# An attention and mixture-of-experts kernel: attention's instruction order written out as a list, and some of its steps moved between engines

## The chip, the cores and the metric

One Trainium2 chip, one of its cores. The metric is device time in microseconds from start to end of one execution, in the median of several runs. The engines named below are PE (TensorE, matrix products and transposes), DVE (VectorE), ACT (ScalarE), POOL (GpSimd) and SP (which here issues most DMAs). Each engine runs its own instructions in program order, and engines wait for one another by semaphores.

## The reference

Two stages. Attention with a memory term, for 8 batches of 8 heads, 576 positions and 64 columns; then a mixture of experts whose tokens are assigned by one global sort.

```python
scores = scale * np.matmul(q, k.transpose(0, 1, 3, 2))
scores = np.where(causal, -1000000000.0, scores)
scores = scores - scores.max(-1, keepdims=True)
a = np.exp(scores)
a /= a.sum(-1, keepdims=True) + 1e-09
local = np.matmul(a, v)
def phi(x):
    return np.where(x > 0, x, np.exp(x) - 1.0) + 1.0
q_p = phi(q)
mem_ret = np.einsum('bhsd,bhde->bhse', q_p, M_prev)
mem_norm = np.einsum('bhsd,bhd->bhs', q_p, z_prev)[..., None] + 1e-06
mem_out = mem_ret / mem_norm
g = 1.0 / (1.0 + np.exp(-beta))[None, :, None, None]
return (g * mem_out + (1 - g) * local).astype(np.float32)
```

The MoE then takes the 4608 rows of 512 columns, gives each to one of 8 experts (at most 576 rows an expert, in the order of the logits) and computes `np.maximum(x[mask] @ w1[e], 0.0) @ w2[e]`.

## The kernel before

Attention works in 16 units, each half a batch: four heads of 576 positions, held as 18 blocks of 128 rows for k, q and phi(q). Most values are kept as two fp16 halves, a high half (a rounded copy) and a low half (what the copy lost), so that a product of two such values is several fp16 matmuls. For each unit `attention` adds steps to a planner:

- loads of k, q, v and M by SP (`lk`, `lq`, `lv`, `lm`);
- `turned` for k, q and phi(q): the high half (`kh`, `qh`, `ph`; a cast of 1152 columns), the low half (`kl`, `ql`, `pl`; a subtraction), transposes on PE into a PSUM bank, and their evacuation to the tiles kT, qT and pT by DVE or ACT (`te`);
- `kb` and `qmove`: copies of kT and qT to other partitions, by DMA;
- `maxes`: raw scores of each block of rows, and their row maxima under the causal mask. Before, DVE adds a mask and takes the maximum in one instruction (`Q`, line 1067, with an accumulator read) for tiles of 512, 384, 256 and 128 columns, and a plain reduction (`R`, line 1066) where no mask is needed; the maxima of a unit are transposed on PE (`mfin2`), copied (`mfin2r`) and moved into the tile qM by DMA (`mfin3`);
- phi(q) in the tile ef: `phr` (a ReLU of -q), `phe` (the exponential, ACT, in place, line 1138), `phs` (max(q, 0) plus it, DVE, line 1139);
- `mz`: z copied into the last column of the M tile mf (line 1142), then M's high and low halves (`mh`, `mh2`, `ml`);
- `vh`, `vl`: v's halves in the tile V;
- `scores`: scores with the maxima subtracted (`S`, PE), exponentials by ACT (`Eh`, `Ef`, `E`), low halves of the exponentials by DVE or POOL (`P2v`, `P2`), products with v and with M (`AV1` to `AV3`, `AVm`), the division and the sum of both terms (`N0` to `N3`, `nadd`), and the result's high and low halves (`ncast`, `nsub`) in the tile xs, which SP stores to HBM and transposes for the logits (`fin`).

Five PSUM banks (`pb`) are shared by transposes, maxima, scores and logits of all units; a step that takes a bank waits for the one that lets it go. The planner `Sched.run` goes through all steps once while the program is made: each has a duration, a priority (the large table `PR`) and one or more engines that may do it, some pinned by `PR['pin']`; it takes at each point the step that can start first, and the resulting order is the order of instructions on every engine. `LK` names steps that are held not to overlap between DVE and POOL; it is used by the planner alone. The MoE (`moe_all`) has a planner run of its own with the table `PM`.

`cp` copies on a chosen engine, and its lines are those of ACT (933), DVE (934) and POOL (935).

Of the kernel before, what the change touches and what calls it, by code (L numbers as in the profile page):

```python
# [23 lines left out]
 'dl': {'0': {'AV': -2321.92,  # L24
              'MX': 1567.76,
              'N': -24421.58,
              'P2': -4357.96,
              'S': 101.14,
              'fin1': 22868.1,
              'fin2': 10356.86,  # L30
              'kb': 10286.06,
              'kh': -45730.44,
              'kl': 20174.46,
              'kt': -4701.95,
              'lk': -12408.59,
              'lm': -8436.44,
              'lq': -2541.36,
              'lv': -3.36,
              'maxrem': 3733.37,
              'mfin': 29276.67,  # L40
              'mfin2': -10538.29,
              'mfin3': 7506.77,
              'mh': -11209.39,
              'ml': -432.1,
              'mz': 12658.92,
              'nadd': -11907.02,
              'ncast': -7225.71,
              'nsub': -10647.97,
              'ph': -1228.79,
              'phe': -9589.46,  # L50
              'phr': 524.92,
              'phs': 2230.42,
              'pl': 4308.28,
              'proc24': 3267.06,
              'pt': 11255.13,
              'qh': -4155.4,
              'ql': 7002.13,
              'qmove': -223.83,
              'qt': 10808.21,
              'sj4': 22053.16,  # L60
              'vh': -293.15,
              'vl': -4289.79},
        '1': {'AV': -11630.65,
              'MX': 5085.57,
              'N': -6291.91,
              'P2': -3722.96,
              'S': 0.29,
              'fin1': 18360.27,
              'fin2': -6498.84,
              'kb': -13149.86,  # L70
              'kh': -9834.86,
              'kl': -14831.77,
              'kt': 2765.98,
              'lk': -26.17,
              'lm': -31.5,
              'lq': -62.5,
              'lv': 65.33,
              'maxrem': 241.19,
              'mfin': 827.99,
              'mfin2': 5904.98,  # L80
              'mfin3': 8067.82,
              'mh': -6693.41,
              'ml': -3921.85,
              'mz': 12321.27,
              'nadd': 28446.8,
              'ncast': -5424.62,
              'nsub': -11693.87,
              'ph': 492.03,
              'phe': 2716.39,
              'phr': -7873.98,  # L90
              'phs': -15036.85,
              'pl': 8602.27,
              'proc24': -8298.99,
              'pt': 9687.89,
              'qh': 27462.53,
              'ql': -726.83,
              'qmove': -2093.73,
              'qt': -7770.46,
              'sj4': 1.71,
              'vh': -3758.76,  # L100
              'vl': -4489.33},
        '10': {'AV': 2861.92,
               'MX': 0.01,
               'N': -4207.12,
               'P2': -7603.6,
               'S': -0.44,
               'fin1': -11796.22,
               'fin2': 2697.91,
               'kb': -6760.73,
               'kh': -7032.06,  # L110
               'kl': 9191.09,
               'kt': -2885.08,
               'lk': -23037.77,
               'lm': -3438.56,
               'lq': -2491.39,
               'lv': -3392.66,
               'maxrem': 7.99,
               'mfin': -13621.83,
               'mfin2': -3709.75,
               'mfin3': -12679.91,  # L120
               'mh': 4128.87,
               'ml': 4639.23,
               'mz': -8635.19,
               'nadd': 14785.77,
               'ncast': 20932.03,
               'nsub': 12672.19,
               'ph': 3299.99,
               'phe': -9809.36,
               'phr': -20534.33,
               'phs': -933.81,  # L130
               'pl': 8303.64,
               'proc24': 9747.88,
               'pt': -5727.95,
               'qh': 56.16,
               'ql': -21808.29,
               'qmove': -6139.71,
               'qt': 813.03,
               'sj4': -16488.77,
               'vh': 2047.99,
               'vl': -16738.43},  # L140
        '11': {'AV': -11203.75,
               'MX': 0.6,
               'N': 14876.06,
               'P2': -700.32,
               'S': 0.11,
               'fin1': -8124.01,
               'fin2': -3919.93,
               'kb': 9923.63,
               'kh': 12644.97,
               'kl': -13145.41,  # L150
               'kt': -4241.87,
               'lk': -6151.58,
               'lm': -7286.77,
               'lq': 7551.39,
               'lv': 7510.93,
               'maxrem': 2.79,
               'mfin': 22015.1,
               'mfin2': 6463.64,
               'mfin3': -7945.76,
               'mh': -9010.16,  # L160
               'ml': 7934.19,
               'mz': -3520.69,
               'nadd': 2187.16,
               'ncast': 12966.79,
               'nsub': -4987.87,
               'ph': 4067.79,
               'phe': 16439.48,
               'phr': -16517.7,
               'phs': 7862.4,
               'pl': 3996.54,  # L170
               'proc24': 2350.4,
               'pt': -0.15,
               'qh': 1067.34,
               'ql': 512.84,
               'qmove': -18712.55,
               'qt': -9981.91,
               'sj4': -4091.57,
               'vh': -11967.99,
               'vl': -5668.57},
        '12': {'AV': 13431.14,  # L180
               'MX': -0.34,
               'N': 6485.25,
               'P2': -2957.52,
               'S': 0.54,
               'fin1': -4378.18,
               'fin2': 23705.86,
               'kb': -1628.06,
               'kh': -4672.12,
               'kl': 9427.26,
               'kt': -3533.86,  # L190
               'lk': -3255.11,
               'lm': 3597.42,
               'lq': 2527.1,
               'lv': 5090.06,
               'maxrem': 0.14,
               'mfin': -7530.28,
               'mfin2': -24054.29,
               'mfin3': -4992.24,
               'mh': 2100.24,
               'ml': 10776.14,  # L200
               'mz': -6507.17,
               'nadd': 6833.95,
               'ncast': -7937.44,
               'nsub': -4335.52,
               'ph': -18163.77,
               'phe': -21792.72,
               'phr': 5627.57,
               'phs': -4855.84,
               'pl': -1558.07,
               'proc24': -9941.83,  # L210
               'pt': -18765.17,
               'qh': 5798.81,
               'ql': -1106.61,
               'qmove': 10262.54,
               'qt': -7534.44,
               'sj4': -7761.78,
               'vh': -14193.73,
               'vl': -14434.34},
        '13': {'AV': -8356.88,
               'MX': -0.87,  # L220
               'N': -7818.18,
               'P2': 5237.25,
               'S': -1.37,
               'fin1': -6282.38,
               'fin2': -13271.62,
               'kb': -7142.61,
               'kh': 3724.27,
               'kl': 3441.14,
               'kt': 9439.61,
               'lk': 2207.4,  # L230
               'lm': 10938.95,
               'lq': 4829.3,
               'lv': -23324.49,
               'maxrem': 5.14,
               'mfin': 4464.01,
               'mfin2': -357.39,
               'mfin3': 4612.32,
               'mh': -2791.23,
               'ml': -11716.33,
# [636 lines left out]
def attention(ctx,tc,q,k,v,M_prev,z_prev,beta,wg,xd,L1,NB,cst,rcst):  # L876
# [98 lines left out]
    def one(nm,alts,f,p,**kw): return SC.add(nm,alts,f,prio=c0+p,**kw)  # L975
# [799 lines left out]
```

## Time and profile before

| | |
|---|---|
| median of three runs | 911.14 us (910.07 to 912.41) |
| the profiled execution | 910.64 us, its span 908.8 us |
| mean granted TensorE clock | 0.959 |
| busy over the span: PE, DVE, ACT, POOL | 803.3, 670.7, 580.7, 543.7 us |
| attention, search, MoE | 0 to about 437, to about 480, to the end |

Busy times are unions of the drawn intervals. A matmul's end is modelled, and successive matmuls overlap, so PE's busy time is not its work. In the groups, the first number behind the bar is the busy time of a group in us, the second the mean of one instruction in ns, and then comes the idle time of the engine just ahead of these instructions with what ended it.

### The profile page before, as it was taken

The numbers are of one execution on the slowest core, as the hardware profiler recorded it, in microseconds if no ns is written. First come the engines' busy times: TensorE is split into PE (matmuls) and PEld (weight loads), VectorE is DVE, ScalarE is ACT, GpSimd is POOL, SyncE is SP. The second block draws the span as 40 slices with busy tenths as digits, with TensorE's granted clock in tenths as the row PEclk, the third lists the DMA queues.
The fourth block names the chain that finished last, engine by engine and source line by source line (L and its number), as shares of the span: only waits on it lengthen the run. The fifth ranks groups of instructions, "written<-read, shape, count | busy, mean of one in ns | idle before, by whom it ended". The sixth has DMA issues, their size and how long they took to land.

```text
span 908.8 us, 24389 instructions
## 1 busy us (share of the span) xinstructions
PE 803.3 (88%) x9240; PEld 526.2 (58%) x9240; DVE 670.7 (74%) x2507; ACT 580.7 (64%) x1027; POOL 543.7 (60%) x564
## 2 busy tenths in 40 slices
PE   3687998999999899999226999999999999999995
PEld 2475887777787688888115445454444444444442
DVE  8798898999999899997788878787867774111020
ACT  4767787887898888976226674848383846552120
POOL 5776886887898786866104492928174646852101
PEclk9999899999999999999557999999999999999998
DMA  5566777765757566334124455566463828940001
GB/s 127 117 142 132 166 155 156 165 149 127 161 130 168 120 139 136 86 71 92 48 93 146 164 144 195 143 213 148 167 168 124 226 89 208 248 150 18 35 13 41
DMA packets 231755, 120.86 MB, mean 133 GB/s; under 512 B 199509, under 2 KB 208725, under 8 KB 231637
## 3 DMA queue, kind: packets, MB, share of 16 engines
q1 hardware_dynamic: 225749, 100.42, 45.2%
q0 software_dynamic: 5888, 18.88, 6.7%
q8 instruction: 72, 1.18, 0.5%
q14 instruction: 46, 0.38, 0.1%
HBM read 72.40 MB, written 18.87 MB: 100 GB/s over the span
## 4 chain that ended last, share of the span: by engine, by line
PE 49%; DVE 22%; issue 12%; DMA 6%; POOL 5%; ACT 3%; SPq 2%; another core or an unknown queue 0%; POOLq 0%; DVEq 0%; ACTq 0%
PE py L1417 15%; PE ph L1417 15%; PE pb L892 7%; PE avo L892 5%; DVE pb L1067 4%; DVE scr L1658 2%; DVE xt L1264 2%; DMA xT<-xs 2%; PE pb L1052 2%; PE prem L1417 2%; DVE pl L1210 2%; SPq L959 1%; POOL h L1043 1%; PE pr L1417 1%; DMA qM<-qT 1%
## 5 line engine op out<-in xcount | busy, mean ns | idle before, releaser
L1574 POOL TENSOR_TENSOR wl<-wst,wh 128x1024 f16<-128x1024 f32 x62 | 131.3, 2140 | 80.8 <-ACT wh L1573 59.5
L1417 PE MATMUL ph<-xT,wh 128*128 128x512 f16 (+1 forms) x560 | 162.9, 364 | 2.8 <-DVE hl L1617 1.4
L1067 DVE CUSTOM_DVE_ANT_0 pb<-pb,maskF 128x128 f32<-128x128 f32 (+3 forms) x256 | 124.7, 497 | 7.4 <-PE pb L892 3.7
L892 PE MATMUL pb<-qT,kT 128*128 128x64 f16 (+3 forms) x576 | 106.1, 245 | 8.2 <-DVE mx L1067 1.8
L1636 POOL DMA_INDIRECT out_dram<-ys,idx x40 | 38.9, 973 | 119.1 <-ACT ys L1631 99.8
L1205 ACT ACTIVATE ph<-pb 128x512 f16<-128x512 f32 x144 | 86.0, 597 | 29.1 <-PE pb L892 23.0
L1617 DVE SCALAR_TENSOR_TENSOR hl<-ph,hh 128x512 f16<-128x512 f32 x64 | 44.0, 688 | 80.2 <-ACT hh L1616 77.2
L1417 PEld LDWEIGHTS <-wh 128*128 128x128 f16 x1072 | 68.4, 98 | 59.6 <-issue 3.5
L892 PE MATMUL pb<-qM,kB 128*128 128x64 f16 (+3 forms) x576 | 99.2, 244 | 1.7 <-DMA qM<-mr 1.7
L1417 PE MATMUL py<-wh,hh 128*128 128x512 f16 x256 | 97.0, 379 | 1.5 <-ACT hh L1616 1.1
L1417 PE MATMUL ph<-xT,wl 128*128 128x512 f16 (+1 forms) x280 | 97.7, 363 | 0.0
L1417 PE MATMUL py<-wl,hh 128*128 128x512 f16 x256 | 97.0, 379 | 0.0
L1417 PE MATMUL prem<-xT,wh 128*128 128x64 f16 x512 | 96.3, 193 | 0.0
L1658 DVE TENSOR_SCALAR_CACHE_REDUCE scr<-p_LwT,th 128x320 f16<-128x320 f32 x168 | 85.1, 543 | 2.7
L1616 ACT ACTIVATE hh<-ph 128x512 f16<-128x512 f32 x64 | 38.0, 593 | 76.2 <-PE ph L1417 55.5
L892 PE MATMUL pb<-kT,qM 128*128 128x512 f16 (+5 forms) x384 | 77.6, 314 | 8.8 <-DVE mx L1067 3.4
L1417 PEld LDWEIGHTS <-hh 128*128 128x128 f16 x512 | 47.3, 97 | 56.2 <-ACT hh L1616 1.3
L1656 ACT ACTIVATE scs<-p_LwT,th 128x320 f16<-128x320 f32 x84 | 47.0, 560 | 50.7 <-DVE th L1665 40.2
L892 PE MATMUL avo<-V,ph 128*128 128x65 f16 x1344 | 78.7, 194 | 0.0
L892 PE MATMUL avo<-V,pl 128*128 128x65 f16 x672 | 74.9, 196 | 0.0
L892 PEld LDWEIGHTS <-ph 128*128 128x128 f16 x1344 | 70.6, 98 | 5.1 <-issue 0.9
L1496 POOL DMA_INDIRECT xg<-xd,idx x40 | 38.6, 964 | 51.6 <-DVE sa L1517 35.0
(304 smaller groups left out, 2358.3 us busy)
## 6 DMA issues: line engine op xcount, KB each, us to landing
wst<-in_moe_w_dram SPq DMA_DIRECT2D x32, 1024.0 KB, 7.7
kf<-in_k_dram SPq DMA_DIRECT2D x64, 128.0 KB, 2.8
qf<-in_q_dram SPq DMA_DIRECT2D x64, 128.0 KB, 2.8
xd<-xs SPq DMA_DIRECT2D x16, 512.0 KB, 3.5
vf<-in_v_dram SPq DMA_DIRECT2D x48, 128.0 KB, 2.8
kB<-kT SPq DMA_DIRECT2D x15, 288.0 KB, 3.4
qM<-qT SPq DMA_DIRECT2D x15, 288.0 KB, 5.5
vF<-in_v_dram SPq DMA_DIRECT2D x16, 128.0 KB, 3.1
```

The lines of the kernel that those rows point to most:

```text
L892: def MM(*a,**kw): mm(*a,skip_group_check=True,**kw)
L1052: for i in range(a,b_): nc.tensor.transpose(p[:,128*(i-a):128*(i-a)+128],g()[:,i],cst['idh'])
L1067: Q=lambda o,i,n: nc.vector.tensor_tensor_reduce(out=i,in0=i,in1=cst['maskF'][:,512-n:512],scale=1.0,scalar=-3e38,op0=ALU.add,op1=ALU.max, ...
L1205: c=SC.add('Eh',[('A',478)],lambda x,a=a: nc.scalar.activation(phs_[x.buf['ph']][:,0:512],pbb[a.buf['pb']],AF.Exp,scale=0.125),acq=('ph',) ...
L1417: def MM(*a,**kw): mm(*a,skip_group_check=True,**kw)
L1496: SC.add('gather',[('P',1250 if i<4 else 1200,'p',0,(1250,'n'))],lambda x: G_.indirect_dma_start(out=xg[0:r_,i],out_offset=None,in_=xd,in_ ...
L1574: SC.add('sp',[('P',2079)],lambda x,ws=ws,k=k,s=s: G_.tensor_sub(wl[:,k,s],ws(),wh[:,k,s]),r=[key+('h',)],w=[key+('l',)],after=[b],rel=rel ...
L1616: b=SC.add('hh',[('A',478)],lambda x,a0=a0,f=f: A_.activation(hh[:,f],phb[a0.buf['ph']],AF.Relu),w=[('hh',f)],after=[y],prio=pr('hh',n,pos ...
L1617: SC.add('hl',[('V',602)],lambda x,a0=a0,f=f: V_.scalar_tensor_tensor(hl[:,f],phb[a0.buf['ph']],0.0,hh[:,f],op0=ALU.max,op1=ALU.subtract), ...
L1636: SC.add('scat',[('P',1250 if i<4 else 1200,'p',0,(1250,'n'))],lambda x,e=e,i=i,r_=r_: G_.indirect_dma_start(out=outv[5*n+i],out_offset=ba ...
L1656: SC.add('sign',[('A',547)],lambda x,j=j,t_=t_,c_=c_: A_.activation(scs[j-KV],LwT,AF.Sign,bias=t_[:,4:5],accum_out=c_[:,j:j+1]),r=['LwT',( ...
L1658: V(462,lambda x,j=j,t_=t_,c_=c_: V_.tensor_scalar(scr[j],LwT,t_[:,j+1:j+2],0.0,op0=ALU.is_ge,op1=ALU.add,accum_out=c_[:,j:j+1]),r=['LwT', ...
```

## The change

The large table of offsets and priorities for attention is emptied, and so are the pins. A list `PR_ORDER` of 3118 step numbers takes their place, with one digit for each step that more than one engine may do (355) and one for each buffer taken (1166); `Sched.given` follows it, checking that every step's inputs come earlier. Beside that:

- **maxima**: the tiles of 384+128 and 256+256 columns get their mask by an added matmul (`mk`, identity times mask, 128 columns) and are reduced by plain reductions, the two of 256 by one instruction; the tile of 512 columns stays as it was;
- **phi**: the exponential goes to PSUM banks in pieces of 512, 512 and 128 columns (unit 0: by its two parts), and `phs` reads them from there;
- **engines allowed**: from unit 1 on, DVE may no longer do `kh`, `qh`, `ph`, `vh`, low halves, `kb`, `qmove`, `phr`, `nsub`, `mz`, `mh`, `mh2`, `ml`;
- names `do` and `dm` stand for the two views of the divisors that were written out before;
- planner durations are changed, which a given order doesn't use.

Read against the order in which steps are added, the digits give from unit 1 on: `kh` 11 times ACT and 4 POOL; `qh` 12 ACT and 3 POOL; `ph` 12 ACT and 3 POOL; `vh` 7 ACT and 8 POOL; `kb` 14 DMA and 1 ACT, `qmove` 15 DMA; evacuations of 1024 columns 49 DVE and 41 ACT, of 256 columns 31 DVE and 14 ACT; `mfin2r` 4 DVE and 11 ACT; `ncast` with unit 0 11 DVE, 33 ACT and 20 POOL. In the kernel before (`ph` on DVE; `kh`, `qh`, `vh` on ACT) evacuations of 1024 and 256 columns on DVE were 52 and 44, and `ncast` 3 DVE, 59 ACT and 2 POOL.

The core of the diff (the tables and the list cut):

```diff
- 'pin': {'kb': 'd',
...
+ 'pin': {},
...
+PR_ORDER = ('''
+5 21 2 23 26 4 22 25 0 24 1 28 27 3 32 31 41 30 43 42 29 45 6 44 47 248 46 49 48 246 57 51 111 50 239 59 53 245 52 61 238 114 58 9 112 115 63 241 60 116 243 10 64 65 244 67 70 247 66 117 12 242
...
+    def given(self,ids,alts,bufs):
+
+        al,bu=[iter(''.join(x.split())) for x in (alts,bufs)]; free={k:set(range(v)) for k,v in self.pools.items()}; out=[]
+        for i in map(int,ids.split()):
+            x=self.n[i]; a=x.alts[int(next(al)) if len(x.alts)>1 else 0]; x.eng=a[0]; x.var=a[2] if len(a)>2 else None
+            assert all(d.start is not None for d in x.deps)
+            for p in x.acq: x.buf[p]=int(next(bu)); free[p].remove(x.buf[p])
+            for p,o in x.rel: free[p].add(o.buf[p])
+            x.start=len(out); out.append(x)
+        assert len(out)==len(self.n)
+        return out
...
+            rq=MK(u)+[('qMz',u%3)]; mk=lambda o: MM(o,identb,maskM,start=False,stop=True)
...
-                        MM(p[:,0:384],qT[:,4*h+2],kq(h,3),start=True,stop=True)
-                        MM(p[:,384:512],qT[:,4*h],kq(h,1),start=True,stop=True)
-                    def f2(p,h=h): Q(mx[:,4*h+2:4*h+3],p[:,0:384],384); Q(mx[:,4*h:4*h+1],p[:,384:512],128)
...
+                        MM(p[:,0:384],qT[:,4*h+2],kq(h,3),start=True,stop=False); mk(p[:,256:384])
+                        MM(p[:,384:512],qT[:,4*h],kq(h,1),start=True,stop=False); mk(p[:,384:512])
+                    def f2(p,h=h): R(mx[:,4*h+2:4*h+3],p[:,0:384]); R(mx[:,4*h:4*h+1],p[:,384:512])
...
+                        h=2*h2+y; o=p[:,256*y:256*y+256]; MM(o,qT[:,4*h+1],kq(h,2),start=True,stop=False); mk(o[:,128:256])
+                def f2(p,h2=h2): R(mx[:,8*h2+1:8*h2+8:4],p.rearrange('p (a b) -> p a b',b=256))
...
+            for c0_ in range(a,b_,8):
+                c1_=min(c0_+8,b_); n=n64(c0_,c1_); pv=lambda x,n=n: pbb[x.buf['pb']][:,0:n].rearrange('p (t d) -> p t d',d=64)
+                y=SC.add('phe',[('A',75+.81*n)],lambda x,a=c0_,b_=c1_,UE=u%NE,pv=pv: nc.scalar.activation(pv(x),ef[UE][:,a:b_],AF.Exp,scale=-1.0),r=K('ef',u%NE,c0_,c1_),acq=('pb',),prio=pr('phe',u))
+                SC.add('phs',[('V',Vt(n))],lambda x,a=c0_,b_=c1_,U2=U2,UE=u%NE,pv=pv,y=y: nc.vector.scalar_tensor_tensor(ef[UE][:,a:b_],qf[U2][:,a:b_],0.0,pv(y),op0=ALU.max,op1=ALU.add),r=K('qf',U2,c0_,c1_),w=K('ef',u%NE,c0_,c1_),after=[y],rel=[('pb',y)],prio=pr('phs',u))
...
-        SC.add('mz',al('mz',u,a=97,v=75),lambda x,u=u,U2=U2: cp(x.var,mf[U2][:,:,64],zT[0:64,4*u:4*u+4]),r=['zT'],w=[('mf',U2,2)],prio=pr('mz',u))
...
+        SC.add('mz',al('mz',u,a=90),lambda x,u=u,U2=U2: cp(x.var,mf[U2][:,:,64],zT[0:64,4*u:4*u+4]),r=['zT'],w=[('mf',U2,2)],prio=pr('mz',u))
...
+            do=lambda: dv(0,5)
+            dm=lambda: dv(5,10)
...
-    order=SC.run(**P_.get('run',{}))
+    order=SC.run(PR_ORDER)
```

## Rows read from the trace of the kernel before

**Rows 1.** Windows: stretch, length, busy us of each engine, clock, DMA share.

```profile
110.00:415.00 305.00, 287.86 (x5001) 240.53 (x4998) 287.46 (x940) 259.14 (x470) 245.29 (x256) 0.99 0.62 135
0.00:437.00 437.00, 385.68 (x6409) 319.10 (x6409) 395.88 (x1276) 342.72 (x614) 333.95 (x421) 0.98 0.60 133
437.00:480.00 43.00, 8.40 (x60) 4.67 (x60) 36.29 (x204) 13.52 (x32) 3.40 (x4) 0.50 0.21 70
```

**Rows 2.** Timeline of PE near 202 us: start us, us, instruction.

```profile
202.07 0.22 PE L892 MATMUL pb<-maskT,identb 128*128 128x128 bf16 x1
202.13 0.19 PE L892 MATMUL pb<-qT,kT 128*128 128x64 f16 x1
```

**Rows 3.** Waits of weight loads, 110 to 415 us: us in total, times, longest.

```profile
PEld L892 <- issue: 22.4, 61, 2.1
PEld L892 <- DMA xT<-xs: 3.2, 4, 2.4
PEld L892 <- DMA qM<-qT: 2.8, 1, 2.8
```

**Rows 4.** The same view, 0 to 110 us.

```profile
PEld L892 <- issue: 14.9, 36, 1.5
...
PEld L1052 <- POOL h L1043: 7.4, 4, 3.2
```

**Rows 5.** Groups of DVE by shape, 0 to 437 us.

```profile
L1067 DVE CUSTOM_DVE_ANT_0 pb<-pb,maskF 128x384 f32<-128x384 f32 x64 | 35.9, 562 | 0.6 <-PE pb L892 0.3
L1067 DVE DVE_READ_ACCUMULATOR2_ANT mx<- 128x1 f32 x256 | 35.9, 140 | 0.0
...
L1067 DVE CUSTOM_DVE_ANT_0 pb<-pb,maskF 128x256 f32<-128x256 f32 x64 | 27.7, 434 | 1.1
...
L1066 DVE TENSOR_REDUCE mx<-pb 128x1 f32<-128x512 f32 x32 | 21.4, 672 | 0.0
L1139 DVE SCALAR_TENSOR_TENSOR ef<-qf,ef 128x1152 f32<-128x1152 f32 x15 | 20.6, 1371 | 0.0
L1067 DVE CUSTOM_DVE_ANT_0 pb<-pb,maskF 128x128 f32<-128x128 f32 x64 | 19.2, 299 | 2.2
L934 DVE COPY pT<-pb 128x1024 f16<-128x1024 f16 x23 | 15.4, 675 | 0.3 <-PE pb L1052 0.3
L934 DVE CAST p<-ef 128x1152 f16<-128x1152 f32 x15 | 14.1, 940 | 0.0
...
L934 DVE COPY mf<-zT 64x4 f32<-64x4 f32 x15 | 11.7, 778 | 0.0
...
L1066 DVE TENSOR_REDUCE pb<-pb 128x2 f32<-128x128 f32 x15 | 4.2, 282 | 0.4 <-PE pb L892 0.4
L934 DVE COPY qT<-pb 128x256 f16<-128x256 f16 x15 | 4.2, 280 | 1.9 <-PE pb L1052 1.8
...
L934 DVE CAST xs<-xt 128x320 f16<-128x320 f32 x3 | 1.4, 478 | 0.0
```

**Rows 6.** Instructions on the tile mf: shortest, median, longest ns.

```profile
L934 DVE COPY mf<-zT x15: 101/611/2308, 24.5 to 370.0; 64x4 f32<-64x4 f32 x15
L933 ACT COPY mf<-zT x1: 181/181/181, 19.9 to 19.9; 64x4 f32<-64x4 f32 x1
```

**Rows 7.** Groups of ACT by shape, 0 to 437 us.

```profile
L933 ACT CAST xs<-xt 128x320 f16<-128x320 f32 x59 | 26.9, 456 | 11.8 <-POOL xt L1272 10.6 <-DVE xt L1278 1.0
...
L933 ACT CAST h<-qf 128x1152 f16<-128x1152 f32 x15 | 17.3, 1153 | 7.1 <-DMA qf<-in_q_dram 5.5 <-issue 1.5
...
L933 ACT CAST V<-vf 128x960 f16<-128x960 f32 x15 | 15.3, 1018 | 4.0 <-PE avo L892 4.0
```

**Rows 8.** Groups of POOL by shape, 0 to 437 us.

```profile
L1280 POOL TENSOR_TENSOR xs<-xt,xs 128x320 f16<-128x320 f32 x64 | 50.6, 798 | 13.9 <-ACT xs L933 13.6
...
L1043 POOL TENSOR_TENSOR h<-kf,h 128x640 f16<-128x640 f32 x15 | 21.0, 1397 | 0.0
...
L935 POOL TENSOR_SCALAR h<-qf 128x640 f16<-128x640 f32 x1 | 0.7, 722 | 2.5 <-DMA qf<-in_q_dram 2.5
```

More of the change, by code (lines that the diff above doesn't have):

```diff
@@ L649 @@
+ 'dl': {},
  'e_phh': 'a',
@@ L762, in add, with run @@
         self.n.append(x); return x
-    def run(self,tol=100,sem=170,same=110,t0=0.0,hwg=450,dlat=1300,dend=950,ph=2800.0,thr=3060,pel=60):
+    def given(self,ids,alts,bufs):
[8 more added lines that the diff above has]
+        return out
+    def run(self,order=None,tol=100,sem=170,same=110,t0=0.0,hwg=450,dlat=1300,dend=950,ph=2800.0,thr=3060,pel=60):
+        if order: return self.given(*order)
         N=len(self.n)
@@ L988, in f @@
         for y in vf: nc.gpsimd.memset(y[64:128,RB:NVT:2],0.0); nc.gpsimd.memset(y[0:64,RB+1:NVT:2],0.0)
-    one('avz',[('P',3000)],f,-150,w=['avz']+[('vf',i,x_) for i in range(2) for x_ in range(RB,NVT)])
+    one('avz',[('P',4300)],f,-150,w=['avz']+[('vf',i,x_) for i in range(2) for x_ in range(RB,NVT)])
     one('bt',dq(23),lambda x: nc.sync.dma_start(out=bt,in_=bass.AP(tensor=beta.tensor,offset=beta.offset,ap=[[0,128],[1,8]])),-188,w=['bt'])
@@ L997, in f @@
         for i in range(10): V_.tensor_scalar(eps[:,:,i],gt[:,:,i//5],(1e-9,1e-6)[i//5]/256,None,op0=ALU.mult)
-    one('gt',[('V',700)],f,-155,r=['bt'],w=['gt'])
+    one('gt',[('V',1300)],f,-155,r=['bt'],w=['gt'])
     for i in range(2):
@@ L1006, in f @@
             put(129,g0); nc.gpsimd.tensor_sub(cl4[i][:,0:NHd],g0[:,0:NHd],V16[i][:,0:RB,129].rearrange('p (h t) -> p h t',t=4)[:,:,0]); put(64,cl4[i])
-        one('put',[('P',1150)],f,-154+20*i,r=['gt'],w=[('V16g',i)])
+        one('put',[('P',1900)],f,-154+20*i,r=['gt'],w=[('V16g',i)])
     for i in range(NVF):
@@ L1093, in f @@
                     for y in range(2):
-                        h=2*h2+y; o=p[:,256*y:256*y+256]; MM(o,qT[:,4*h+1],kq(h,2),start=True,stop=True)
-                def f2(p,h2=h2):
-                    for y in range(2): Q(mx[:,8*h2+4*y+1:8*h2+4*y+2],p[:,256*y:256*y+256],256)
-                part('MX',f,f2,512,218,672,[('qM',u%3,8*h2+1),('qM',u%3,8*h2+5)]+kk,(h2,2),x0+4.5)
+                        h=2*h2+y; o=p[:,256*y:256*y+256]; MM(o,qT[:,4*h+1],kq(h,2),start=True,stop=False); mk(o[:,128:256])
+                def f2(p,h2=h2): R(mx[:,8*h2+1:8*h2+8:4],p.rearrange('p (a b) -> p a b',b=256))
+                part('MX',f,f2,768,335,600,[('qM',u%3,8*h2+1),('qM',u%3,8*h2+5)]+kk,(h2,2),x0+4.5)
                 def f(x,h2=h2):
@@ L1100, in f @@
                     for y in range(2): MM(p[64*y:64*y+64],qT[:,16+h2,64*y:64*y+64],kq(2*h2+y,4),start=True,stop=True)
-                part('MX',f,lambda p,h2=h2: R(mx[:,16+h2:17+h2],p),1024,339,598,[('qM',u%3,16+h2)]+kk,(h2,3),x0+5)
+                part('MX',f,lambda p,h2=h2: R(mx[:,16+h2:17+h2],p),1024,220,598,[('qM',u%3,16+h2)]+kk,(h2,3),x0+5)
             for gi,G in enumerate(gs):
@@ L1306, in lg @@
                     for c in range(2): MM(lo[:,i,0:8],xT[:,i,2+c],wgs[:,2*hf+c,0:8],start=False,stop=c==1)
[L1307 removed]
+            a=SC.add('lg',[('T',545)],lg,wg=240,r=['wgs'],after=tl+ch('lg'),acq=('pb',),rel=[('xT',t)],prio=pr('fin2',u)); ch('lg',a)
             lt=lts[b%2]; V_=nc.vector
```

764 lines of the change are left out of this document (37 added, 727 removed), and 84 rows, old and new, of the table PR_ORDER.

## The prediction

> **What bounds the kernel now.** I read the engines' busy time by stretch first, then the waits, then the groups of instructions by shape, and last a few rows in order of time for spacing. The stretches [rows 1] split the span in three: attention up to about 437 us, a search of 43 us in which PE works 8.4 us, and the MoE. The diff touches attention alone, so what it can give or take is what those 437 us become; MoE and search follow at the same length. In the body of attention (110 to 415 us) DVE is busy 287.5 of 305 us and PE 287.9, ACT 259.1, POOL 245.3. Over the whole of attention DVE has the most: 395.9 of 437 us.
>
> PE's figure has to be read with care. A mask step of 128 columns is drawn 0.22 us long, but the next matmul starts 0.06 us after it [rows 2]: busy intervals overlap and cover short waits. PE's weight loads show the waits better: in the body they sat idle 31.8 us in long waits, of which the three largest kinds are shown (six smaller ones make 3.4 us), and in the first 110 us 41.4 us in nine kinds, two of them shown [rows 3, 4]. Only 2.8 and 3.2 us of the body's waits have a DMA behind them; most read "issue" (the in-order queue of PE standing at a matmul whose bank or operand isn't there). PE's own work in attention is therefore at most 364 us (437 less 73), and DVE with 396 us is the engine that sets the pace: banks come free and operands arrive as fast as DVE empties them. So I price the change by what it takes from DVE, and then ask whether PE can use it.
>
> **The change part by part.** Counts of engines come from reading the list's digits against the order in which the steps are added (the section on the change has them). A unit is half a batch, 16 in all.
>
> *Memory copies.* 15 of 16 copies of z into the M tile leave DVE for ACT. Four columns, yet 778 ns a copy, 11.7 us in all [rows 5]; one takes 101 ns at best and 2308 at worst [rows 6], so nearly all of it is waiting while holding DVE. DVE: -11.7. On ACT the one copy there took 181 ns [rows 6]: 15 times that is +2.7.
>
> *Phi's high half.* 15 casts of 1152 columns at 940 ns leave DVE [rows 5]: -14.1. Twelve go to ACT at the 1153 ns of the same cast of q [rows 7], +13.8; three to POOL.
>
> *Masks.* Per unit 12 PE mask steps are added, 8 for the 384+128 tiles and 4 for the 256+256 ones: 192 in all, 0.06 us each by the spacing of [rows 2], +11.5 us of PE. Bounds: nothing if all fall into PE's waits, 42 us at the drawn 0.22. On DVE 64 masked maxima each of 384, 256 and 128 columns go (35.9+27.7+19.2 = 82.8 us [rows 5]). In come 64 reductions of 384 (between 282 ns at 128 columns and 672 at 512, on a line 542), 64 of 128 and 32 of 512: 34.7+18.0+21.5 = 74.2. DVE: -8.6. The accumulator reads that belong to masked maxima (140 ns, 192 of 256 go, 27 us) I leave out, since they are drawn over the next instruction's start, as PE's are; they are the other end.
>
> *Phi's exponential.* One ACT pass in place becomes three into PSUM banks, one DVE sum of 1371 ns becomes two of 512 columns and one of 128 that read PSUM. At the reductions' prices that is 2 x 672 + 282 = 1626 ns: 15 x 0.255 = +3.8 on DVE; on a pure line for 1152 columns (282 + 8/3 x 390 = 1322) it would be -0.7, the other end. ACT gets two more starts per unit, at 181 ns each +5.4. It also takes a PSUM bank three times per unit, which is a rival below. [...] No row of the trace has this very sum from PSUM.
>
> *Other moves between engines.* 3 of 52 evacuations of 1024 columns (675 ns; three rows of that kind, one shown) and 13 of 44 of 256 columns (280 ns, likewise) leave DVE: -5.7 [rows 5]. Eight more result casts come to it (478 ns): +3.8. Four of the transposed maxima come at 280 ns: +1.1. ACT loses 4 + 3 casts of k and q (1153), 8 of v (1018) and 26 result casts (456), -28.1 [rows 7], and gets 16 evacuations, +9.0 at the rows of v's and the result casts. POOL gets 10 casts of 1152 columns, 8 of 960 and 18 of 320; by its one cast of 640 columns, 722 ns [rows 8], taken in proportion: 13.0+8.7+6.5 = +28. [...]
>
> *What does nothing.* Low halves on GpSimd: outside unit 0 they are there already (the row of h<-kf in [rows 8] has all 15). Separate result tiles: the diff has none; two new names give the same views as before. Both cost nothing either way, and nothing hides them.
>
> *The order.* Each engine's program becomes a written list instead of the planner's choice. Nothing in the trace prices that; it decides how much of PE's 73 us of waits goes. From below, it could make them longer.
>
> **The sum.** Attention's busy time becomes DVE 395.9 - 31.4 = 364.5; PE's own work at most 364 + 11.5 = 375; POOL 334 + 28 = 362; ACT 342.7 + 2.8 = 345.5. No engine stands out any more. If DVE alone set the pace and its 41 us of idle time stayed, the end would come 31.4 us earlier, 879 us. But with four engines within 30 us of one another, each wait for one holds the next, and PE has 11.5 us more to do. I take it that of the 31.8 us of waits in the body six tenths end (19), because those hang on DVE's banks, and of the 41.4 us at the start a fifth (8), because most of that waits for the first loads and low halves of units 0 and 1. 27 - 11.5 = 15.5 us. The profiled execution took 910.64 us (span 908.8 and 1.8 around it), 0.5 below the median of the three runs: 910.64 - 15.5 = 895.1 us, with 887 to 903 as this case's own range. In the search and the MoE nothing moves.
>
> **The rivals.**
> A, a larger gain: the order lets DVE's relief through whole, PE's waits in the body all but end, and attention comes near DVE's new load plus today's 41 us: 910.64 - 31.4 = 879, and anything under 887 counts as this case. For it: DVE is busy in 94% of the body. Against it: PE, POOL and DVE now need the same time.
> B, no change: the waits take another form. Phi's exponential takes three of five shared banks in every unit, each for an ACT pass and a DVE sum; if each of the 48 takings holds a group of matmuls back by 0.3 us, that is 15 us and the gain is gone: 908 to 913. For it: "issue" heads PE's waits, so banks are short now. Against it: the same banks are let go sooner by shorter maxima.
> C, slower: POOL becomes the bound. It has 334 us to do in 437 and idles 103, because its inputs come late (13.6 us before the low halves of results for their ACT cast [rows 8]). With 362 us it needs its idle time to fall to 75 for attention to stay at 437. From there on each microsecond of idle that stays is lost; if 85 stay, attention takes 447, and the time is 920. Place: low halves of k, q and phi now queue behind casts on POOL, and transposes on PE wait for them. For it: [rows 4] has PE waiting 7.4 us for POOL's low halves. Against it: the order can put those casts where POOL waits today.
> D, a change that doesn't do what it says: the two parts that do nothing have no time, and the rest is plain in the diff; no case of its own.
>
> **How the numbers follow.** A measurement of this kernel tells apart about 0.3%, 2.7 us: faster is under 907.9, slower over 913.4. The forecast (887 to 903) 0.48; A (879 to 887) 0.16, and beyond it 0.03; a part of the gain (903 to 908) 0.13; B 0.11; C 0.09. So faster 0.80, same 0.11, slower 0.09. The range leaves out what lies beyond A and most of B and C: 880 to 909, which takes in the open ends of the masks and of phi's sum.
>
> **What would show it.** Right: attention's end moves from 437 to about 421; the M copy on ACT takes under 0.3 us and DVE's group of it is gone; DVE's busy time in attention is near 365 and POOL's near 362; PE's weight loads wait some 20 us less in the body; search and MoE keep their length to 2 us. Wrong: PE's waits as long as before with new rows for phi's banks (B), or PE waiting for POOL's low halves and POOL idle under 75 us with attention over 437 (C). A MoE of another length would mean that I missed something that the order of attention hands on, such as when the last stores land.

## The result and the profile after

The changed kernel takes 899.64 us (median of 4 runs, 897.5 to 900.57) beside 911.09 for the kernel before: a ratio of 0.987, 95% interval 0.9848 to 0.9893, or 11.5 us less where 15.5 had been forecast. Its profiled execution took 900.57 us, span 898.5.

| in the two traces, us from the start | before | after | difference |
|---|---|---|---|
| last matmul of the memory term (`avm`) | 431.9 | 419.0 | -12.9 |
| first count of the search | 442.4 | 430.0 | -12.4 |
| first matmul of the MoE | 484.4 | 472.2 | -12.2 |
| end of the span | 908.8 | 898.5 | -10.3 |

So in these two traces the whole gain is made in attention, and some 2 us are lost behind it. The engines' busy time by stretch, to be held against [rows 1] (columns as there; attention now ends near 426):

```profile
0.00:110.00 110.00, 89.17 (x1361) 71.61 (x1362) 96.05 (x259) 91.26 (x171) 87.80 (x166) 1.00 0.62 139
110.00:400.00 290.00, 278.52 (x4833) 239.29 (x4831) 249.69 (x731) 243.44 (x458) 249.00 (x275) 0.96 0.64 140
0.00:426.00 426.00, 389.57 (x6618) 331.04 (x6618) 364.90 (x1051) 346.65 (x650) 350.80 (x456) 0.97 0.62 137
426.00:470.00 44.00, 8.66 (x53) 5.02 (x54) 37.34 (x207) 14.97 (x34) 5.00 (x5) 0.50 0.20 65
```

DVE's busy time in attention fell from 395.9 to 364.9 us, yet the end came only 12 us earlier: DVE idled 41 us before and idles 61 now. Two thirds of what DVE was relieved of became idle time. Three other engines are now busy for 347 to 390 us (PE's figure covers short waits: in [rows 2] a matmul drawn 0.22 us long is followed after 0.06), so no engine stands out that could be relieved alone.

DVE's groups by shape in the first 425 us; beside [rows 5], the groups of the masked 384, 256 and 128 columns, of `p<-ef` and of `mf<-zT` are gone, and these stand in their place:

```profile
L480 DVE TENSOR_REDUCE mx<-pb 128x1 f32<-128x384 f32 x64 | 35.1, 549 | 4.1 <-PE pb L306 4.0
...
L480 DVE TENSOR_REDUCE mx<-pb 128x2 f32<-128x512 f32 x32 | 21.9, 684 | 7.4 <-PE pb L306 7.3
...
L554 DVE SCALAR_TENSOR_TENSOR ef<-qf,pb 128x512 f32<-128x512 f32 x32 | 21.4, 678 | 1.1 <-issue 0.5 <-ACT pb L553 0.3
L480 DVE TENSOR_REDUCE mx<-pb 128x1 f32<-128x128 f32 x64 | 17.8, 279 | 0.0
...
L348 DVE CAST xs<-xt 128x320 f16<-128x320 f32 x11 | 5.3, 478 | 1.1 <-POOL xt L689 1.0
L554 DVE SCALAR_TENSOR_TENSOR ef<-qf,pb 128x128 f32<-128x128 f32 x16 | 4.5, 278 | 1.7 <-ACT pb L553 1.6
```

What moved to ACT and to POOL (the same view), beside [rows 6 to 8]:

```profile
L347 ACT CAST p<-ef 128x1152 f16<-128x1152 f32 x12 | 13.9, 1159 | 2.0 <-DVE ef L554 1.7 <-PE pb L466 0.3
L347 ACT COPY mf<-zT 64x4 f32<-64x4 f32 x16 | 3.1, 193 | 0.0
```
```profile
L628 POOL TENSOR_TENSOR pl<-pf,ph 128x512 f16<-128x512 f32 x49 | 56.7, 1158 | 8.7 <-ACT pf L627 8.4
L697 POOL TENSOR_TENSOR xs<-xt,xs 128x320 f16<-128x320 f32 x64 | 50.5, 794 | 6.8 <-ACT xs L347 2.9 <-DVE de L677 1.7 <-DVE xs L348 1.2
...
L349 POOL TENSOR_SCALAR xs<-xt 128x320 f16<-128x320 f32 x20 | 9.2, 460 | 1.2 <-DVE xt L695 0.4
L349 POOL TENSOR_SCALAR V<-vf 128x960 f16<-128x960 f32 x8 | 8.1, 1018 | 5.3 <-PE avo L306 4.9 <-DMA qM<-qM 0.5
```

The long waits of PE's weight loads, first 0 to 110 us, then 110 to 400 us (us in total, times, longest), beside [rows 3, 4]:

```profile
PEld L306 <- issue: 11.9, 25, 1.9
PEld L466 <- DVE h L457: 11.5, 3, 9.9
```
```profile
PEld L306 <- issue: 8.3, 26, 2.2
PEld L306 <- DMA xT<-xs: 6.9, 2, 3.7
PEld L306 <- POOL pl L628: 1.4, 1, 1.4
```

With the smaller kinds these views add up to 28.3 us at the start (41.4 before) and 20.9 in the body (31.8 before): 49.2 instead of 73.2. What went are 17.1 of the 37.3 us of "issue" in the rows shown, and 6.6 of the 7.4 us for POOL's low halves of k and q [rows 4]. The wait of 11.5 us for DVE's low halves, most of it before the first matmul, is old: it was 11.0 us before. The wait for the transposed result (`xT`) doubled, now in two waits of up to 3.7 us: the logits of units 1 and 3 stand in the list at a place that PE reaches before the DMA behind them has landed.

### The profile page after: what moved, and what is told of

The parts are those of the page before. It is cut to its first block, busy times and chain, and to the rows that moved or that the text cites. A ratio compares the mean times of both kernels' runs of the same rounds, so it can differ in the third digit from the quotient of the medians.

```text
span 898.5 us, 24664 instructions
## 1 busy us (share of the span) xinstructions
PE 809.4 (90%) x9432; PEld 539.1 (60%) x9432; DVE 638.4 (71%) x2276; ACT 584.2 (65%) x1062; POOL 561.0 (62%) x599
## 4 chain that ended last, share of the span: by engine, by line
PE 62%; issue 10%; DVE 10%; DMA 6%; POOL 5%; SPq 4%; ACT 2%; another core or an unknown queue 0%; POOLq 0%; DVEq 0%; ACTq 0%
PE py L834 16%; PE ph L834 15%; PE pb L306 13%; PE avo L306 9%; PE pb L466 3%; DVE scr L1075 2%; DMA qM<-qT 2%; PE prem L834 2%; SPq L373 2%; POOL h L457 2%; PE avm L306 1%; DMA xT<-xs 1%; PE pr L834 1%; DMA qf<-in_q_dram 1%; SPq L380 1%
## 5 line engine op out<-in xcount | busy, mean ns | idle before, releaser
L834 PE MATMUL ph<-xT,wh 128*128 128x512 f16 (+1 forms) x560 | 164.8, 368 | 2.9 <-DVE hl L1034 1.4
L480 DVE TENSOR_REDUCE mx<-pb 128x1 f32<-128x512 f32 (+3 forms) x192 | 89.4, 503 | 14.6 <-PE pb L306 14.1
L306 PE MATMUL pb<-kT,qM 128*128 128x512 f16 (+5 forms) x384 | 82.5, 312 | 5.1 <-DMA qM<-qT 2.4
L306 PE MATMUL avo<-V,ph 128*128 128x65 f16 x1344 | 76.7, 193 | 0.0
```

Source lines behind the costliest of these rows:

```text
L306: def MM(*a,**kw): mm(*a,skip_group_check=True,**kw)
L480: R=lambda o,i: nc.vector.tensor_reduce(o,i,axis=mybir.AxisListType.X,op=ALU.max)
L834: def MM(*a,**kw): mm(*a,skip_group_check=True,**kw)
```

## The experiments

Each experiment stands beside runs of the kernel before on the same chip; in three groups of runs, on different chips, these took 912.9, 909.8 and 904.05 us, so ratios are compared and not times (a ratio is not exactly the quotient of the two medians). The changed kernel itself, run once more on another chip:

**after_again** (no edit). 

> The changed kernel once more, so that the three runs beside it stand against it on one chip. All theories: 0.985 to 0.989 of the kernel before.

894.63 beside 904.05: 0.9893 [0.9867, 0.9919]. The gain is 9 to 12 us on either chip, and 0.987 and 0.9893 show how far two measurements of one kernel can lie apart.

### The moves without the order

**old_mz**: the kernel before, only the copies of z on ACT. 

> The kernel before with one thing changed: the z copies that were on DVE are done by ACT, at the same places of the old order. Theory (these copies cost what the change gave back: with them on DVE the changed kernel took as long as the kernel before): DVE loses 11.7 us of waiting, and the time is 900 to 906 us for 911 before. Rival (the written order gives the time, the copies matter only in it): 909 to 913.

```diff
+    for x in SC.n:
+        if x.nm=='mz' and x.var=='v': x.var='a'
```

908.61, ratio 0.9983 [0.996, 1.0006]. The expected 900 to 906 us did not come. DVE's busy time in the body fell from 287.5 to 277.0 us, and nothing that can be told came of it: in this profile PE's long waits up to the last `avm` matmul add up to 73.6 us, against 74.0 before.

**old_moves**: the kernel before with three parts of the change: copies of z and phi's high halves on ACT (`if x.nm in ('mz','ph')` in the same place) and the smaller masks on PE, as in the diff of the change. 

> The kernel before in its old order, with the z copies and phi's high half on ACT and the masks of the smaller maxima on PE; phi's exponential stays as it was. DVE loses 11.7 + 14.1 + 8.6 us, ACT gets 15 x 1.15 + 2.7 = 20 us, PE 11.5. Theory (DVE's relief is what counts): 895 to 903. Rival 1 (only the z copies count): like the run with these alone, 900 to 906. Rival 2 (the old order isn't made for it; ACT becomes late): 906 to 915.

932.84, 1.0237 [1.019, 1.0284]. DVE has 247.0 us to do in the body, 40 less than before, and attention ends 23 us later. The window of the body and the largest waits of this kernel (its first 440 us):

```profile
110.00:415.00 305.00, 276.87 (x4702) 233.67 (x4699) 247.03 (x704) 250.72 (x444) 229.52 (x242) 0.97 0.59 128
```
```profile
PEld L892 <- issue: 37.0, 97, 1.6
DVE pl L1209 <- ACT pb L1208: 24.0, 26, 3.6
...
POOL h L1043 <- ACT h L933: 22.8, 9, 3.8
POOL p4l L1177 <- ACT p4f L1176: 16.1, 6, 6.7
...
POOL p L1043 <- ACT p L933: 14.8, 13, 2.9
```

DVE and POOL wait longer for ACT: in the kernel before, by the same view, the second to fourth of these rows were 5.9, 12.3 and 10.1 us, and the last was no row, as the cast was DVE's. It fits that the casts now stand in ACT's program ahead of exponentials for which DVE and POOL wait; no run moved the casts alone. PE's "issue" is no longer than before (37.5 us). Up to the last `avm` matmul PE's long waits grew from 74.0 to 79.3 us only; the mask steps added some 11.5 us, and PE was at its lower clock (granted clock 0.50) for 23.9 us of attention instead of 13.7, by estimate worth up to 5 us of work: in the trace of the changed kernel the matmuls on `avm` start 30 ns apart at a granted clock of 1.00 (from 129.77 us) and 54 ns apart at 0.50 (from 215.41 us). That is most of the 23 us. So the masks on PE, which cost nothing that can be told in the written order (masks_back below), seem to have been paid for in this one.

**planner_new**: the changed kernel's steps without its list; the planner with the old table of offsets chooses order and engines. 

> The steps of the change (masks on PE, phi's exponential in PSUM, z copies and phi's high halves off DVE) without the written list: the planner of before with its table of priorities orders them; the exponentials of a unit are chained again as before, without which it stands still. Theory (steps and order are worth something only together): 905 to 925 us. Rival (the steps are enough if the order is made with them in mind): within 4 us of the changed kernel.

```diff
- 'pin': {},
+ 'pin': {'kb': 'd',
...
-    order=SC.run(PR_ORDER)
+    order=SC.run(**P_.get('run',{}))
```

(The edit also brings back the old table and pins, and chains a unit's exponentials as before.)

925.61, 1.0228 [1.0198, 1.0258]. DVE's busy time in the body is 259.4 us and in all of attention 368.5, within 4 us of the changed kernel's, and attention ends 33 us later than there (last `avm` matmul 452.0): PE's long waits up to there are 78.7 us, against 49.2, and it was at its lower clock for 41.0 us, against 20.5. The table's numbers were made for other steps, so this shows the moves without a fitting order, not the best that the planner could do.

### The order without the moves

**all_back**: the changed kernel's list, with the copies of z, phi's high halves and the smaller masks on DVE and phi's exponential in SBUF. 

> The changed kernel's written order with the steps as they were before: z copies and phi's high halves of units 1 to 15 on DVE, masks of the smaller maxima on DVE, phi's exponential in SBUF (still in three pieces, with its banks taken). Theory (who does the steps gives the time): DVE gets some 30 us back in an order that wasn't made for it, 912 to 925 us. Rival (the order gives the time): 899 to 905.

```diff
     order=SC.run(PR_ORDER)
+    for x in [y for y in SC.n if y.nm=='mz'][1:]: x.var='v'
+    for x in [y for y in SC.n if y.nm=='ph'][2:]: x.var='v'
```

(and the edits of masks_back and phs_back, below.)

920.63, 1.0105 [1.0048, 1.0162]: DVE's busy time is 415.3 us in the first 440. So the list with these four parts put back loses 1%, the moves without the list lose over 2%, and both together gain 1.3%. This is not the old kernel in a new order: evacuations, result casts and the casts of k, q and v stay where the list puts them, and phi's sum is in three pieces of two SBUF operands, which alone costs more than this 1% (phs_back below). What the list would be worth with the old steps as the old planner kept them, no run shows.

### One part undone at a time, in the changed kernel's order

**mz_back**: the copies of z of units 1 to 15 back on DVE, at the same places of the list. 

> The changed kernel with the z copies of units 1 to 15 on DVE again, at the same places of the list. Theory (DVE's relief is what gave the time): DVE gets back some 15 x 0.78 = 11.7 us of mostly waiting; PE sets the pace now and hides a part, so 902 to 908 us. Rival (the written order alone gave the time, not who does the copy): within 2 us of the changed kernel, 898 to 902, whatever DVE's busy time does.

```diff
     order=SC.run(PR_ORDER)
+    for x in [y for y in SC.n if y.nm=='mz'][1:]: x.var='v'
```

914.42, 0.9995 [0.9959, 1.0032]: with fifteen copies of four columns back on DVE, the whole gain is gone. The tile mf (shortest, median, longest ns), then DVE, POOL and PE in order of time around the longest copy (start us, us, instruction):

```profile
L348 DVE COPY mf<-zT x15: 153/636/5862, 26.8 to 393.4; 64x4 f32<-64x4 f32 x15
```
```profile
205.87 5.86 DVE L348 COPY mf<-zT 64x4 f32<-64x4 f32 x1
211.65 0.20 DVE L682 RECIPROCAL de<-de 128x10 f32<-128x10 f32 x1
```
```profile
205.25 1.15 POOL L457 TENSOR_TENSOR p<-ef,p 128x512 f16<-128x512 f32 x1
206.36 1.39 POOL L457 TENSOR_TENSOR h<-qf,h 128x640 f16<-128x640 f32 x1
207.71 1.53 POOL L697 TENSOR_TENSOR xs<-xt,xs 128x320 f16<-128x320 f32 x2
209.21 1.14 POOL L628 TENSOR_TENSOR pl<-pf,ph 128x512 f16<-128x512 f32 x1
210.32 1.39 POOL L457 TENSOR_TENSOR p<-ef,p 128x640 f16<-128x640 f32 x1
```
```profile
207.15 0.22 PE L306 MATMUL pb<-maskF,identb 128*128 128x128 bf16 x1
212.55 0.37 PE L306 MATMUL pb<-qT,kT 128*128 128x256 f16 x1 [5.18 <-DVE kT L348]
```

The copy ends at 211.73, 20 ns after the last of six POOL instructions that ran back to back: it did not get in between any two of them, and DVE stood for 5.9 us. The fifteen hold DVE 17.1 us in this order (11.7 in [rows 5]). The last row shows how the stall reaches PE: the next matmul needs kT, whose evacuation stood behind the copy on DVE, and PE stood 5.2 us.

Longer waits are not all of the price. The last `avm` matmul ends at 428.0 us, 9.0 later than in the changed kernel, and PE's long waits up to there grew by 4.1 us only (53.3 against 49.2). But PE was at its lower clock for 34.1 us of attention, against 20.5, and 13.6 us more at a granted clock of 0.50 are by the same estimate up to 6.8 us of work. The three longest of these stretches (the figure after POOL's busy time is the granted clock) each begin in, or within 1.5 us of, a long wait of PE: 2.2, 3.0 and 5.3 us.

```profile
118.60:128.80 10.20, 10.20 (x99) 9.51 (x99) 6.13 (x18) 6.20 (x13) 6.05 (x7) 0.50 0.78 170
166.30:173.20 6.90, 6.90 (x60) 5.32 (x56) 3.54 (x13) 3.69 (x7) 3.16 (x4) 0.51 0.77 202
210.70:217.50 6.80, 4.95 (x45) 3.59 (x45) 5.12 (x12) 1.86 (x4) 1.01 (x1) 0.50 0.81 184
```

In the ten executions of this kernel the mean granted clock is 0.949, and in the 17 of the kernel before beside them 0.957. So the price of the copies is in part that of a lower clock, and how the two share it is an estimate. Attention still ends 3.9 us earlier than in the kernel before (431.9); the rest of the loss lies in the MoE (432.3 us in this profile against 426.3), and no run shows that the copies make that part.

**mz_reduce**: as mz_back, but the copy is written as a maximum over one element. 

> The changed kernel with the z copies of units 1 to 15 on DVE, at the same places, but written as a reduction over one element in place of a copy. Theory (a copy between SBUF tiles on DVE waits until GpSimd's running instruction, or a row of them, has ended; a reduction doesn't): these fifteen take some 0.15 us each, and the time is that of the changed kernel within 3 us. Rival (any work on DVE at these places costs, or any read of SBUF by DVE waits): as slow as with the copies, 11 to 15 us above the changed kernel.

```diff
-  cp(x.var,mf[U2][:,:,64],zT[0:64,4*u:4*u+4])
+  nc.vector.tensor_reduce(mf[U2][:,:,64],zT[0:64,4*u:4*u+4,None],axis=mybir.AxisListType.X,op=ALU.max)
```

893.91, 0.9885 [0.9859, 0.9911], the changed kernel's own ratio. Same engine, same place in the list, same values:

```profile
L557 DVE TENSOR_REDUCE mf<-zT x15: 141/144/150, 25.9 to 385.9; 64x4 f32<-64x4 f32 x15
```

So neither the work nor DVE's load is the price of these copies, but the form: this copy between SBUF tiles waited for POOL, up to 5862 ns and 636 in the median, and the reduction didn't, at most 150 ns and 144 in the median.

**phs_back**: phi's exponential in place in SBUF, and the sum reads it there; pieces, banks taken and places as in the changed kernel. 

> The changed kernel with phi's exponential written to SBUF in place and DVE's sum reading it there; pieces, places in the list and banks as in the changed kernel. Theory (a DVE sum of two SBUF operands waits for GpSimd as the z copy does): the sums of 512 columns take 0.75 to 1.2 us for 0.68, and the time is 901 to 906 us. Rival 1 (only the price of reading PSUM changes): 0 to 5 us of DVE less, 896 to 900. Rival 2 (both hidden): 898 to 901.

```diff
- nc.scalar.activation(pv(x),ef[UE][:,a:b_],AF.Exp,scale=-1.0)
+ nc.scalar.activation(ef[UE][:,a:b_],ef[UE][:,a:b_],AF.Exp,scale=-1.0)
- nc.vector.scalar_tensor_tensor(ef[UE][:,a:b_],qf[U2][:,a:b_],0.0,pv(y),op0=ALU.max,op1=ALU.add)
+ nc.vector.scalar_tensor_tensor(ef[UE][:,a:b_],qf[U2][:,a:b_],0.0,ef[UE][:,a:b_],op0=ALU.max,op1=ALU.add)
```

914.78, 1.0047 [1.0027, 1.0067]: slower than the kernel before. Its sums by shape, in the first 440 us:

```profile
L554 DVE SCALAR_TENSOR_TENSOR ef<-qf,ef 128x512 f32<-128x512 f32 x32 | 39.8, 1257 | 1.2 <-POOL xt L689 0.5 <-ACT ef L553 0.3 <-POOL pl L628 0.2
L554 DVE SCALAR_TENSOR_TENSOR ef<-qf,ef 128x128 f32<-128x128 f32 x16 | 15.1, 943 | 1.9 <-ACT ef L553 1.7
```

With both operands in SBUF the same sums hold DVE 54.9 us, with one in PSUM 25.9. The longest takes 5737 ns, over a row of POOL instructions again; with one operand in PSUM the longest takes 689. The waiting goes both ways: the same POOL instructions hold POOL 360.6 us of attention, against 350.8. That is the use of the PSUM banks: it frees the sum of POOL's timing. By the ratios the old form costs some 16 us here, where 2 to 7 were expected. The kernel before got by with 20.6 us [rows 5]. Its planner keeps a set of steps, `phs` among them and `mz` not, that it starts on DVE only when POOL is done, and I take that for the reason; no run took the rule away.

**ph_back**: phi's high halves of units 1 to 15 on DVE (as in mz_back, with `ph` for `mz`). 

> The changed kernel with phi's high halves of units 1 to 15 on DVE again, at the same places of the list. Theory (DVE's relief): DVE gets 15 x 0.94 = 14 us back, ACT loses 12 x 1.15 us and POOL three casts; 902 to 909 us. Rival (order alone): 898 to 902. Rival (ACT and POOL are now the late ones, since POOL and ACT took the casts): faster, 893 to 897.

903.2, 0.9912 [0.988, 0.9944]. The casts take 16.5 us of DVE there, 1097 ns each, and cost 2 to 4 us, if that: the interval overlaps that of the changed kernel.

**masks_back**: the smaller masks on DVE again, by the old masked maxima; 192 PE steps fewer. 

> The changed kernel with the masks of the smaller maxima on DVE again (masked maxima of 384, 256 and 128 columns, no added mask matmuls), at the same places of the list. PE loses 192 x 0.06 = 11.5 us of work, DVE gets 8.6 us by the groups' times. Theory: PE sets the pace now, and its 11.5 us are paid in full where DVE has idle time; so the masks on PE cost more than they give and the time is 890 to 896 us. Rival (DVE still sets it): 902 to 908 us. Rival (both hidden): 898 to 901.

```diff
- def f2(p,h=h): R(mx[:,4*h+2:4*h+3],p[:,0:384]); R(mx[:,4*h:4*h+1],p[:,384:512])
+ def f2(p,h=h): Q(mx[:,4*h+2:4*h+3],p[:,0:384],384); Q(mx[:,4*h:4*h+1],p[:,384:512],128)
...
```

905.28, 0.9914 [0.9879, 0.9949]. The last `avm` matmul ends at 418.6 us, against 419.0 with the masks on PE. PE's long waits in the first 420 us add up to 61.2 us, 12.0 more than in the changed kernel; "issue" is most of it:

```profile
PEld L306 <- issue: 30.8, 82, 2.5
```

DVE is busy 15.3 us more than in the changed kernel, not 8.6 (us from the start, both up to 418.6; first the changed kernel, then masks_back):

```profile
0.00:418.60 418.60, 386.29 (x6549) 328.32 (x6550) 360.63 (x1034) 345.26 (x648) 348.21 (x453) 0.98 0.63 138
0.00:418.60 418.60, 380.43 (x6367) 316.56 (x6368) 375.94 (x1259) 346.41 (x648) 348.72 (x453) 0.99 0.63 138
```

So the 11.5 us of mask steps fill time in which PE stands otherwise. (In this profile PE was at its lower clock for only 6.8 us of attention, against 20.5, so the equal ends flatter masks_back by up to 7 us.) That they cost the time 11.5 us is refuted; whether they bring up to 0.4% stays open, as the intervals overlap.

### The new wait for the logits

**lg_later**: the logits of units 1 and 3 some 40 places later in the list (steps 423 to 425 from place 837 to 875, steps 814 to 817 from 1191 to 1231). 

> The changed kernel with the logits' matmuls of units 1 and 3 some 40 places later in the list, and three bank digits changed for it; nothing else. In the changed kernel PE stood 3.9 us (at 117 us) and 3.2 us (at 166 us) before these matmuls until the transposing DMA of xs had landed, and the granted clock was 0.5 from 127.9 to 138.1 and from 175.6 to 182.5 us, the first stretches after them. Theory: both waits were made by the list alone, and the half clock follows from them; without them 7 us of waiting and 17 us at half clock (8.5 us of work) are saved, and the time is 884 to 888 us. Rival 1: the clock falls for another reason; only the waits go, 892 to 894. Rival 2: PE waits for something else at the same place (DVE or POOL are as late), 898 to 901.

900.36, 0.9888 [0.9838, 0.9938], no faster than the changed kernel. The two waits of 3.7 and 3.1 us are gone (0.5 us for xT is left), but the first count of the search came only 3.4 us earlier (426.6).

The stretches of half clock that the expectation names are misread: from 127.9 to 138.1 and from 175.6 to 182.5 us the granted clock of the changed kernel was 1.00. The lower level lies some 11 us earlier, right around the two waits, and a third time near 213 us. The windows of the changed kernel:

```profile
117.00:127.50 10.50, 10.21 (x89) 8.89 (x90) 5.13 (x16) 5.00 (x10) 5.30 (x6) 0.51 0.83 183
164.90:171.90 7.00, 6.01 (x58) 4.61 (x59) 2.89 (x11) 2.71 (x6) 3.37 (x5) 0.51 0.78 204
212.50:216.50 4.00, 4.00 (x56) 3.69 (x55) 1.83 (x5) 2.74 (x5) 0.00 (x0) 0.57 1.21 173
```

and of lg_later in the first two of them:

```profile
117.00:127.50 10.50, 8.03 (x180) 6.67 (x177) 7.61 (x24) 6.57 (x13) 6.98 (x8) 1.00 0.85 189
164.90:171.90 7.00, 6.78 (x78) 5.98 (x77) 5.34 (x16) 5.60 (x11) 4.17 (x5) 0.85 0.79 212
```

The clock is up there, but by windows of 5 us it was down for 17 us elsewhere (near 25, 48, 82, 135 and 166 us), against 20.5 in the changed kernel. In the changed kernel each of the three stretches begins in, or within 1 us of, a long wait of PE (3.7, 3.1 and 2.2 us); in lg_later four of the five begin within 1.5 us of other waits, of 1.7 to 2.0 us. Two waits of 1.9 and 1.8 us in the changed kernel, up to 46.9 and 80.8 us, have no such stretch behind them. So the low clock did follow these two waits, but it doesn't hang on them: without them it came behind others.

**lg_later_2**: the same kernel, timed beside after_again. 

> The kernel with the logits' matmuls of units 1 and 3 later, again, beside the changed kernel on one chip and in more rounds. If the waits that go are worth something: 3 to 5 us under the changed kernel. If they come back elsewhere: within 2 us of it.

891.68, 0.987 [0.9844, 0.9896], against 894.63. It has the lowest median on this chip; the 3 us are not told apart from nothing.

## Why the prediction was right, and where it was off

**DVE bounds attention, and loses 31 us.** The total came: 364.9 us against 364.5 forecast. In part that is luck. By masks_back the masks alone took 15.3 us off DVE where the sum had 8.6 (the prediction left out the accumulator reads and named them as the other end, 27 us), so the other parts gave some 16 us together and not 22.8. That DVE sets the pace is not borne out by itself: old_mz took 10.5 us off it in the body for nothing that can be told, and planner_new 27 us with a loss. Prices that held: reductions 74.8 us (forecast 74.2; 549 ns at 384 columns, on a line 542), phi's sum 25.9 (24.4 for 15 units, 26.0 with unit 0), result casts at the same 478 ns. The copies of z take 193 ns each on ACT (181).

**Phi's sum from PSUM, +3.8 us.** The size is right; the sum had it as a pure cost. phs_back shows what the step is for: in this order the old form costs 29 us of DVE and 1.8% of the time. I had read waiting out of the copies of z (101 to 2308 ns), and did not ask for it at this sum of two SBUF operands.

**Copies of z, -11.7 us of DVE.** Right in cause (waiting, not work) and too small in weight. In the old order taking them off is worth nothing that can be told (old_mz), in the new one as much time as the whole gain (mz_back). The price of these stalls was not their length on DVE (17.1 us in mz_back): it showed in what PE then waited and in PE's clock. In mz_back's trace the longest "issue" wait of PE grows from 2.2 to 5.3 us, and PE is 13.6 us longer at its lower clock.

**Masks, +11.5 us of PE.** Size right (192 steps), but it is inside PE's waits (masks_back), the lower bound of the prediction. Half right, then: PE's own work is indeed 375 us (424.5, which is 437 less the 12.5 us by which the end moved, less 49.2 of long waits), and yet taking 11.5 us off it brings the end no nearer.

**PE's waits, 27 of 73 us go.** 24.0 went: 10.9 in the body (forecast 19) and 13.1 at the start (forecast 8). At the start, 6.6 us are POOL's low halves of k and q, which no longer come late; in the body, 3.7 of the 8 us that are missing are added waits for transposed results. This is the term that was guessed, six tenths and a fifth, and it is the one that was mis-sized: 24.0 - 11.5 = 12.5 us, beside the 12.4 to 12.9 by which attention's end moved and the 15.5 forecast.

**POOL, 362 us.** Too high: 350.8. The added casts are 10 of 1152 columns (11.6 us), 8 of 960 (8.1) and 18 of 320 (8.3), 28 together as forecast. What was not foreseen is that POOL's old work shrinks by 11 us: unit 0 and the first set-up have other engines or shorter instructions, and the 49 low halves `pl` take 1158 ns instead of the 1217 of the row below. The copies of z are not the reason for the latter: with them back on DVE `pl` takes 1157 ns (mz_back). With phi's sum back in SBUF it takes 1177 (phs_back), and with the sum and phi's casts back on DVE 1218 (all_back), so in this order it is these instructions of DVE that stand in POOL's way. In the old order `pl` falls from 1214 (old_mz) to 1176 ns (old_moves) when phi's casts, with the masks, are off DVE. ACT came as forecast, 346.6 us for 345.5.

```profile
L1213 POOL TENSOR_TENSOR pl<-pf,ph 128x512 f16<-128x512 f32 x49 | 59.6, 1217 | 10.3 <-ACT pf L1212 8.2 <-issue 1.8
```

(POOL by shape in the kernel before, 0 to 437 us.) Rival C had no ground: POOL's low halves of results, which waited 13.6 us for ACT [rows 8], wait 2.9 now. Nor had B, banks that phi's exponential takes: PE's "issue" waits fell from 37.3 to 20.2 us.

**Search and MoE keep their length.** From the MoE's first matmul to the end it is 426.3 us, 1.9 more than before: inside the 2 us, but it took a sixth of the gain. The MoE is the same in all kernels of this study, and on one chip this length lies between 426.8 (lg_later) and 432.3 us (mz_back) in the profiled executions, so the 1.9 us can't be put down to the change. In the two traces PE stayed at its lower clock for the first 4.3 us of the MoE before and the first 6.8 after, and once more for 3.4 us after; that alone could be the 1.9 us.

**The granted clock.** Not in the prediction at all. PE was at the lower level for some 14 us of attention before and 20.5 after. Seven microseconds more at a granted clock of 0.50 are by estimate up to 3.5 us of work, nearly as much as the forecast missed; but in after_again it was some 14 us with a like gain, and in lg_later 17. Most of these stretches begin in or just behind a wait of PE, so an order that makes PE wait may pay twice: mz_back had PE's long waits of 53.3 us and 34.1 us at the lower clock, planner_new 78.7 and 41.0. What lowers the clock no run shows, and whether the change itself has a part in it stays open.

**The order, "nothing prices it".** This was the weakest step: the forecast took for granted that the order turns two fifths of PE's waits into time. The runs price it: without a fitting order the moves lose 2.3 to 2.4%, and on one chip the list is worth 31.0 us, 3.4% (planner_new 925.61, after_again 894.63).

## What to carry to other kernels

Relief of the busiest engine is worth what the order lets the others do with it: with four engines within a tenth of one another, the same moves cost 2% in one order and gain 1% in another, so measure moves and order together and one part undone at a time in the new order. Look at the spread of a small instruction, not its mean: the copy of four columns that took 101 to 2308 ns was waiting, and writing it in a form that didn't wait (141 to 150 ns) was worth as much as moving it to ACT (0.9885 and 0.9893 of the kernel before). Ask where the operands of a two-operand sum on DVE lie when POOL is busy beside it: here it took up to 5737 ns with both in SBUF, and at most 689 with one in PSUM.

## What the runs showed of the hardware

- A DVE copy of four columns stood through six back-to-back POOL instructions (5.86 us) and ended 20 ns after the last; a DVE sum of two SBUF tiles took up to 5.74 us (512 columns, mean 1257 ns), against at most 689 ns (mean 678) with one operand in PSUM. In both cases the row of POOL instructions was not broken by the waiting DVE instruction. POOL pays too: 360.6 us for the work of 350.8 where phi's sums read two SBUF tiles.
- The same values by a reduction over one element took 141 to 150 ns in all fifteen, with POOL busy for 350.6 of 426 us.
- ACT's exponential of 512 columns out of PSUM took 602 ns where it went back to PSUM and 598 where it went to SBUF. Out of SBUF it took 604 ns into PSUM (the changed kernel) and 633 in place (phs_back).
- PE's granted clock fell from 1.00 to 0.50 in several stretches of 3.4 to 10 us within attention, at other places in each kernel's profile, and mostly in or just behind a long wait of PE (1.7 to 5.3 us in the traces of the changed kernel, mz_back and lg_later); not every such wait had one behind it.
